# Attention and a split feed-forward on one core: order of a product's terms, tile starts on 128 bytes, a new program order

## The chip, the core and the metric

The kernel runs on one core of a Trainium2 chip. The core has TensorE (PE in the profile; its weight loads are shown apart as PEld), VectorE (DVE), ScalarE (ACT), GpSimd (POOL) and SyncE (SP, which here only issues transfers). The metric is the device time of one execution in microseconds, the median of a few runs. Before the change it was 241.62 us (three runs: 240.11, 241.62 and 242.28).

## The reference

What is computed, cut to its core. The attention is linear: both queries and keys are turned into products of two small projections, keys and values are summed once per batch, and queries read that sum. Its output, put together over heads, runs through a feed-forward with a squared relu.

```python
batch, n_heads, seq, head_dim, r = 4, 4, 1088, 32, 8      # 4352 tokens of 128 values
def phi(x):
    a = np.einsum('rd,bhsd->bhsr', S1, x)
    b = np.einsum('rd,bhsd->bhsr', S2, x)
    return np.einsum('bhsi,bhsj->bhsij', a, b).reshape(*x.shape[:-1], r * r)
q_p, k_p = (phi(q), phi(k))
kv = np.einsum('bhsf,bhsd->bhfd', k_p, v)
z = np.sum(k_p, axis=2)
num = np.einsum('bhsf,bhfd->bhsd', q_p, kv)
den = np.einsum('bhsf,bhf->bhs', q_p, z)[..., None] + 1e-06
x = (num / den), heads side by side                        # 4352 x 128
h = x @ w_in                                               # w_in 128 x 2048
g = s * np.maximum(h, 0.0) ** 2 + b
out = g @ w_out                                            # w_out 2048 x 128
```

## The kernel before

**Tiles.** Everything is held with the 128 features on the partitions and tokens along the free dimension. The 4352 tokens are cut into nine tiles (`TILES`): tile 0 of 256 tokens, tiles 1 to 8 of 512. The 2048 hidden columns are cut into eight pairs (`NPAIR`) of two blocks of 128.

**Keys.** `kvphase(b)` (k0 to k3 in the program order, one per batch) projects the keys (L247), transposes them on DVE (L251), multiplies the two projections (L254), sums keys times values on PE (L268), copies the sum (`kvt`), turns it (L283) and copies it to `st`.

**Queries.** `direct_features` (q0, q1) and `stored_features` (q2 to q8) make the query products `pq`; the latter go through DRAM (`qd`) to be spread over partitions. `attend(t)` (n0 to n8) multiplies them with `st` (L368), divides by the denominator on DVE (L381 to L397) and leaves the tile `x`. For tiles 1 to 8 it is split into a rounded part `xh` and the rest `xl`, both in fp32r, a form of fp32 that PE takes in one pass.

**Weights.** `split_weights` (w0 to w7, w0 the first 512 columns of `w_in`, w1 the first 512 rows of `w_out`, and so on by turns) turns 64-bit numbers from DRAM into fp32 in four steps, `to_float`: two scalings (L115/L117 and L121/L123, on DVE or ACT), a join and a sign step on DVE (L187, L183). The result, `w24`, is then split into large and small parts: `wih` and `wil` of `w_in`, `woh` and `wol` of `w_out`.

**Feed-forward.** `ffn(t, jp)` (the tokens 00 to 87 in the program order: tile, pair) has two matmul blocks. The first, hp, multiplies two weight blocks with x: for tiles 1 to 8 three fp32r matmuls each (small weights with `xh`, large weights with `xh`, large weights with `xl`), six in all, of 128x512. Then the tile `u` is made: relu out of PSUM (L129 on ACT or L127 on DVE), square (L135 or L133), rounding to `uh` (L111, either engine), and the rest `ul` = u - uh (L440, always DVE). The second block, ops, adds both weight blocks' three products into the output's PSUM tile, which is held over all eight pairs: `wol` with `uh`, `woh` with `uh`, `woh` with `ul`. Tile 0 is computed with fp32 matmuls, unsplit. `finish` (L500, L502) scales and stores a tile.

**Buffers.** hp has two PSUM buffers (`ps_h`), `u` two, `uh` and `ul` three each. A matmul stands in PE's program order and waits there for what it reads; DVE and ACT, too, work in program order.

**What sets the order.** `ORDER` is a table of tokens. Each names a generator (a load `L..`, `s`, k, q, n, w, a feed-forward pair, or `z`, one bf16 matmul that only keeps PE busy) and runs it up to its next `yield`. The table thus fixes every engine's order and the order of transfers on SP's queue. `ON_DVE` names the steps that run on DVE and not on ACT: a letter for the step (r relu, q square, u rounding to `uh`, x rounding to `xh`, w.. a weight step, a, b, k copies) and the place.

**Where tiles lie.** Tiles of the pool `const` lie one behind another in SBUF in the order in which they are made, then the pools p1, p2, p3 and p4. `sk` (80 fp32 numbers, 320 bytes for each partition) is followed by `sq`, `srep`, `kvt`, the four split weight tiles, `bias`, the eight `w24` and `s_bits` (320 bytes again). All of those after `sk` begin 64 bytes past a multiple of 128; after `s_bits` the two odd halves add up, and `st` and all tiles of p1 to p4 (`u`, `uh`, `ul`, `x`, `xh`, `xl` among them) begin on multiples of 128.

Of the kernel before, what the change touches and what calls it, by code (L numbers as in the profile page):

```python
# [19 lines left out]
P = 128  # L20
# [14 lines left out]
DEN_APART = (0,)  # L35
FIRST_F32 = (0, 1, 2, 3, 4, 5, 6, 7)
ORDER = """
Ls Lk0 Lk0 Lq0 Lk0 s s Lv0 s s Lv0 s z z z z z z k0 s s Lv0 k0 Lcst k0 z k0 Lq1 q0 q0 Lq2 k0 q0 Lw3 k0 z k0
Lw0 Lw1 k0 k0 z k0 Lw2 k0 q0 q0 Lw4 q0 k0 Lw6 Lw5 q1 k0 k0 q1 Lq4 k0 q1 q2 k0 q1 Lq3 q1 w3 q2 q1 w3 z n0 n0 n0
q2 w0 n0 n0 w0 n0 n0 n0 Lk1 w1 w0 z z z z z n1 w1 w0 Lw7 w3 w2 z 00 w2 w1 01 00 w1 Lq6 00 w2 01 00 w2 Lv1 01  # L40
w3 02 w4 n1 w4 n1 01 Lv1 02 n1 w4 w6 03 02 w6 w4 02 03 w5 w3 03 04 q2 w5 w6 03 Lk1 w0 04 q2 w6 q2 05 w5 04 w1
06 w5 05 w0 04 w6 w7 05 n1 07 n1 06 n1 05 06 n1 w3 n1 k1 w1 w7 q3 07 n1 10 07 w7 Lv3 q3 w7 w4 q3 11 k1 w7 w4
w5 06 w2 w2 07 10 k1 k1 07 07 12 10 k1 07 k1 q3 k1 10 q3 q3 11 Lk2 k1 Lk2 10 10 k1 Lv2 k1 11 Lv2 12 k1 11 14
k1 11 12 11 12 w5 q2 14 13 12 14 12 14 13 n2 14 13 15 w6 13 n2 n2 16 n2 13 15 15 n2 13 n2 n2 15 n2 17 w7 16 15
14 n2 16 17 15 n2 16 q3 20 17 16 Lk3 17 16 20 17 21 20 23 20 Lv3 21 17 20 21 23 22 17 Lk3 21 23 20 17 21 23 21
22 23 24 22 25 22 24 22 24 22 25 24 23 25 24 24 25 n3 25 25 n3 n3 n3 26 n3 n3 n3 27 26 n3 q4 26 n3 k2 n3 q4
Lq5 30 27 26 Lq7 q4 26 27 26 k2 30 k2 k2 30 31 k2 q4 27 30 q4 32 30 q4 30 k2 27 k2 32 k2 31 32 27 k2 32 k2 34
31 27 k2 32 27 31 33 k2 31 34 31 33 34 32 34 33 35 34 33 36 33 35 33 35 q4 36 35 34 35 n4 36 35 n4 36 n4 n4 37
n4 36 36 n4 37 n4 n4 37 q5 n4 k3 n4 37 41 k3 q5 37 q5 37 41 k3 42 37 41 37 40 q5 42 41 q5 q5 41 42 43 42 40 k3
42 q7 40 45 k3 43 40 q6 k3 43 44 q6 40 q7 q6 40 45 q7 41 q5 45 43 q6 42 q6 q6 43 45 n5 45 44 43 q7 44 n5 q7 n5  # L50
46 q7 n5 n5 44 n5 47 n5 46 n5 44 n5 k3 46 n5 q6 k3 46 47 50 46 k3 47 k3 44 50 45 50 47 46 50 47 47 50 50 q7 47
47 k3 51 k3 52 51 51 53 52 51 n6 52 51 51 52 53 n6 54 n6 53 n6 n6 52 55 53 54 n6 52 53 54 56 55 n6 55 53 54 54
54 55 56 57 55 56 n6 55 57 n6 n6 57 56 62 56 56 57 62 57 61 62 60 61 62 61 64 62 n7 61 60 61 57 60 n7 64 60 63
Lq8 60 57 60 57 64 63 61 n7 63 n7 n7 n7 62 n7 n7 64 n7 65 n7 64 66 63 65 q8 63 63 66 65 64 q8 66 65 q8 67 66
66 70 65 q8 65 q8 70 67 67 q8 66 67 70 71 67 70 67 70 72 71 67 71 70 72 67 71 73 72 71 72 71 73 q8 75 72 73 n8
73 72 75 73 75 n8 74 n8 n8 75 n8 n8 73 74 75 76 74 n8 n8 n8 74 77 76 74 74 76 n8 76 81 77 76 75 77 81 82 77 81
80 77 81 76 81 80 77 80 82 82 80 85 80 77 83 77 82 82 80 83 85 83 81 83 82 85 84 83 85 86 85 84 84 87 86 84 83
84 84 86 87 85 87 86 86 87 86 87 87 87 87 87 87
"""
# [30 lines left out]
def attn_ffn_kernel(ctx: ExitStack, tc: tile.TileContext, qT, kT, vp, s80, cst, w_in, w_out, outT):  # L90
    nc = tc.nc
    PSUM = bass.MemoryType.PSUM
    const = ctx.enter_context(tc.tile_pool(name="const", bufs=1))
# [115 lines left out]
    s_col = cst_sb[:, CS:CS + 1]  # L209
    b_col = cst_sb[:, CB:CB + 1]  # L210
    spread = cst_sb[:, CT:CT + P]
    sk = const.tile([P, NS], F32, name="sk")
    sq = const.tile([P, 64], F32, name="sq")
    srep = const.tile([P, 2, 64], F32, name="srep")

    def s_phase():
        bits = const.tile([P, NS], I32, name="s_bits")
        yield from to_float("s", sk, s_raw, bits)
        own = sk[:, 64:].rearrange("p (w r) -> p w r", w=2)
        nc.vector.tensor_copy(out=srep[:, 1].rearrange("p (i x) -> p i x", i=R),  # L220
                              in_=own[:, 1].unsqueeze(1).broadcast_to([P, R, R]))
# [222 lines left out]
    def product(out, terms, first=True, last=True):
        for k, (w, x) in enumerate(terms):
            nc.tensor.matmul(out, w, x, start=(first and k == 0), stop=(last and k == len(terms) - 1))  # L446

    def ffn(t, jp):
        _, N, _ = tiles[t]
        single = t == 0 and jp in FIRST_F32  # L450
        W = N + 2 if t == 0 else N
        hp = ps_h.tile([P, 2, 512], F32, name="hp")
        for i in range(2):
            c, c24 = columns(2 * jp + i)
            if single:
                product(hp[:, i, :N], ((w24[jp // 2, 0][c24], x_first[0]),))
            else:
                xh, xl = (x[:, :N] for x in xhl[t])
                product(hp[:, i, :N], ((wil[:, c], xh), (wih[:, c], xh), (wih[:, c], xl)))
        yield  # L460
        u = p2.tile([P, 2, NMAX], F32, name="u")
        if t == 0:
            nc.gpsimd.tensor_copy(out=u[:, :, N:W], in_=b_col.unsqueeze(2).broadcast_to([P, 2, 2]))
        relu(f"r{t}{jp}", u[:, :, :N], hp[:, :, :N])
        yield
        squared(f"q{t}{jp}", u[:, :, :N], u[:, :, :N])
        yield
# [109 lines left out]
```

## Time and profile before

| what | value |
|---|---|
| median of three runs | 241.62 us |
| profiled execution, whole | 241.27 us |
| its span, first to last instruction | 239.5 us |
| PE busy | 233.2 us, 97% of the span |
| DVE busy | 201.2 us, 84% |
| ACT busy | 174.5 us, 73% |
| granted TensorE clock, mean | 0.997 |

Sums and differences below are made against the profiled execution (241.27 us; 1.77 us of it lie outside of the span). It stands 0.35 us under the median. In the rows, L446 is the helper `product`, which issues every feed-forward matmul, and L111 the helper `copy`, so groups are told apart by the tiles' names: `hp<-xh,wil` is the first block, `ops<-ul,woh` the second. A matmul of fp32 (not fp32r) shows as two records.

### The profile page before, as it was taken

The numbers are of one execution on the slowest core, as the hardware profiler recorded it, in microseconds if no ns is written. First come the engines' busy times: TensorE is split into PE (matmuls) and PEld (weight loads), VectorE is DVE, ScalarE is ACT, GpSimd is POOL, SyncE is SP. The second block draws the span as 40 slices with busy tenths as digits, with TensorE's granted clock in tenths as the row PEclk, the third lists the DMA queues.
The fourth block names the chain that finished last, engine by engine and source line by source line (L and its number), as shares of the span: only waits on it lengthen the run. The fifth ranks groups of instructions, "written<-read, shape, count | busy, mean of one in ns | idle before, by whom it ended". The sixth has DMA issues, their size and how long they took to land.

```text
span 239.5 us, 4351 instructions
## 1 busy us (share of the span) xinstructions
PE 233.2 (97%) x1752; PEld 178.7 (75%) x1752; DVE 201.2 (84%) x262; ACT 174.5 (73%) x206; POOL 3.9 (2%) x15
## 2 busy tenths in 40 slices
PE   7999999999999999999999999999999999999993
PEld 3647877878887778877767887888687877888782
DVE  3679999999677899998998684999899896799882
ACT  2198986989987276856778976865955689987571
POOL 1000110000000000000000000000000000000000
PEclk9999999999999999999999999999999999999998
DMA  6999934870020053100356732000010510001001
GB/s 164 362 414 394 224 95 103 174 269 3 0 88 0 5 155 86 44 0 3 114 150 161 138 79 88 4 0 0 0 47 22 153 66 3 0 0 45 0 3 44
DMA packets 9812, 22.15 MB, mean 92 GB/s; under 512 B 1088, under 2 KB 3520, under 8 KB 9792
## 3 DMA queue, kind: packets, MB, share of 16 engines
q1 hardware_dynamic: 9792, 21.87, 30.7%
q8 instruction: 14, 0.23, 0.4%
q14 instruction: 6, 0.05, 0.1%
HBM read 18.72 MB, written 3.15 MB: 91 GB/s over the span
## 4 chain that ended last, share of the span: by engine, by line
PE 95%; DVE 2%; DMA 1%; ACT 1%; issue 0%; ACTq 0%; DVEq 0%
PE ops L446 41%; PE hp L446 40%; PE psa L368 4%; PE psa L268 4%; PE psa L247 2%; PE psa L327 2%; PE hp L307 1%; PE psa L283 1%; PE ops L512 1%; DMA s_raw<-s 1%; DVE w L187 0%; ACT u L129 0%; DVE pq L316 0%; ACT ot L500 0%; DVE rr L390 0%
## 5 line engine op out<-in xcount | busy, mean ns | idle before, releaser
L440 DVE TENSOR_TENSOR ul<-u,uh 128x1024 fp32r<-128x1024 f32 x64 | 77.9, 1221 | 12.7 <-ACT uh L111 10.2
L129 ACT ACTIVATE u<-hp 128x1024 f32<-128x1024 f32 (+1 forms) x62 | 60.0, 968 | 30.4 <-DVE ul L440 14.6
L135 ACT ACTIVATE u<-u 128x1024 f32<-128x1024 f32 (+1 forms) x53 | 53.6, 1012 | 8.7 <-DVE u L127 7.3
L446 PE MATMUL hp<-xh,wil 128*128 128x512 f32 x128 | 51.5, 402 | 0.0
L446 PE MATMUL ops<-uh,wol 128*128 128x512 f32 x128 | 51.1, 400 | 0.0
L446 PE MATMUL ops<-uh,woh 128*128 128x512 f32 x128 | 50.2, 392 | 0.0
L446 PE MATMUL hp<-xl,wih 128*128 128x512 f32 x128 | 50.2, 392 | 0.0
L446 PE MATMUL hp<-xh,wih 128*128 128x512 f32 x128 | 50.1, 392 | 0.0
L111 ACT CAST uh<-u 128x1024 fp32r<-128x1024 f32 x35 | 36.5, 1048 | 6.5 <-DVE u L133 3.3
L446 PE MATMUL ops<-ul,woh 128*128 128x512 f32 x128 | 39.9, 393 | 0.0
L446 PEld LDWEIGHTS hp<-xh,wil 128*128 128x128 f32 x128 | 24.0, 188 | 7.9 <-ACT u L129 1.4
L446 PEld LDWEIGHTS ops<-uh,wol 128*128 128x128 f32 x128 | 24.0, 188 | 7.5 <-issue 1.8
L446 PEld LDWEIGHTS hp<-xl,wih 128*128 128x128 f32 x128 | 24.0, 188 | 5.5
L446 PEld LDWEIGHTS ops<-ul,woh 128*128 128x128 f32 x128 | 23.8, 188 | 5.7 <-DVE ul L440 0.3
L446 PEld LDWEIGHTS ops<-uh,woh 128*128 128x128 f32 x128 | 24.1, 188 | 4.9
L446 PEld LDWEIGHTS hp<-xh,wih 128*128 128x128 f32 x128 | 24.1, 188 | 4.7
L111 DVE CAST uh<-u 128x1024 fp32r<-128x1024 f32 x29 | 20.0, 691 | 4.0 <-ACT u L135 3.1
L133 DVE TENSOR_TENSOR u<-u 128x1024 f32<-128x1024 f32 (+1 forms) x19 | 22.1, 1164 | 0.2
L127 DVE TENSOR_SCALAR u<-hp 128x1024 f32<-128x1024 f32 x10 | 12.2, 1223 | 4.1 <-PE hp L446 3.6
L254 DVE TENSOR_TENSOR ph<-kab 128x768 f32<-128x768 f32 (+2 forms) x9 | 11.0, 1221 | 0.2
L368 PE MATMUL psa<-pq,st 64*32 64x256 f32 (+3 forms) x320 | 10.2, 345 | 0.5 <-DVE x L397 0.5
L346 DVE TENSOR_TENSOR pq<-pq,br 128x1024 f32<-128x1024 f32 x7 | 8.5, 1220 | 2.0 <-DMA br<-qd 1.9
(63 smaller groups left out, 178.6 us busy)
## 6 DMA issues: line engine op xcount, KB each, us to landing
pq<-qd SPq DMA_DIRECT2D x7, 512.0 KB
br<-qd SPq DMA_DIRECT2D x14, 256.0 KB
qt<-qT SPq DMA_DIRECT2D x8, 256.0 KB
raw<-w_out SPq DMA_DIRECT2D x4, 512.0 KB
raw<-w_in SPq DMA_DIRECT2D x4, 512.0 KB
outT<-ot SPq DMA_DIRECT2D x7, 256.0 KB
vt<-vp SPq DMA_DIRECT2D x3, 330.0 KB
kt<-kT SPq DMA_DIRECT2D x3, 320.0 KB
```

What stands on the lines that cost most here:

```text
L111: (nc.vector.tensor_copy if key in ON_DVE else nc.scalar.copy)(out=out, in_=in_)
L127: nc.vector.tensor_scalar(out=out, in0=in_, scalar1=0.0, scalar2=None, op0=ALU.max)
L129: nc.scalar.activation(out=out, in_=in_, func=AF.Relu)
L133: nc.vector.tensor_tensor(out=out, in0=in_, in1=in_, op=ALU.mult)
L135: nc.scalar.activation(out=out, in_=in_, func=AF.Square)
L247: nc.tensor.matmul(ps[32 * q:32 * q + 32, w * w32:(w + 1) * w32], sk[:, 32 * w:32 * w + 32], kt[:, a:a + w32], start=(w == 0), stop=(w == ...
L254: nc.vector.tensor_tensor(out=ph[:, c0:c0 + n].rearrange("p c h i x -> p (c h) i x"), in0=a.unsqueeze(3).broadcast_to([P, H * n, R, R]), i ...
L268: nc.tensor.matmul(kvp[64 * g:64 * g + VW, 64 * j:64 * j + 64], v_in[b][:, c, h], ph[:, c, h].rearrange("p i x -> p (i x)"), start=(c == 0 ...
L346: nc.vector.tensor_tensor(out=pq, in0=pq, in1=br, op=ALU.mult)
L368: nc.tensor.matmul(out[32 * h:32 * h + 32, e0:e1], st_t[b][64 * r:64 * r + 64, h // 2, h % 2, y], pq[64 * r:64 * r + 64, h, e0:e1], start= ...
L440: nc.vector.tensor_tensor(out=ul[:, :, :N], in0=u[:, :, :N], in1=f32(uh[:, :, :N]), op=ALU.subtract)
L446: nc.tensor.matmul(out, w, x, start=(first and k == 0), stop=(last and k == len(terms) - 1))
```

## The change

Three things. The three products of a weight block are issued in another order in both blocks: small weights with the large stream, large weights with the small stream, then both large; in the second block this goes weight block by weight block, where before both products with `ul` stood last. `sk` and `s_bits` get 96 columns in memory (384 bytes) of which 80 are used, so that every tile of const and of the pools begins on a multiple of 128 bytes. And `ORDER` and `ON_DVE` are new: 745 tokens for 746 (one z fewer; all else the same set), and 70 steps on DVE for 71 (among the large ones 15 relus for 10, 17 squares for 17, 28 roundings to `uh` for 29).

```diff
-Ls Lk0 Lk0 Lq0 Lk0 s s Lv0 s s Lv0 s z z z z z z k0 s s Lv0 k0 Lcst k0 z k0 Lq1 q0 q0 Lq2 k0 q0 Lw3 k0 z k0
...
+z z z z z z z z Ls Lk0 Lq0 Lk0 Lcst s s Lk0 s s Lv0 s s s Lv0 k0 Lv0 q0 Lq1 q0 k0 k0 k0 Lw0 Lq2 k0 Lw2 k0 z k0
...
 ON_DVE = frozenset("""
-a8 k20 k21 k31 q02 q03 q11 q16 q31 q32 q33 q36 q41 q54 q62 q64 q65 q70 q71 q80 q81 q85 q86 r11 r23 r25 r26 r33
...
+a4 a6 b00 k01 q02 q10 q12 q13 q21 q34 q45 q51 q53 q63 q65 q67 q71 q72 q80 q81 q85 q86 r15 r21 r23 r24 r31 r42
...
-    sk = const.tile([P, NS], F32, name="sk")
+    sk = const.tile([P, 96], F32, name="sk")[:, :NS]
...
-        bits = const.tile([P, NS], I32, name="s_bits")
+        bits = const.tile([P, 96], I32, name="s_bits")[:, :NS]
...
-                product(hp[:, i, :N], ((wil[:, c], xh), (wih[:, c], xh), (wih[:, c], xl)))
+                product(hp[:, i, :N], ((wil[:, c], xh), (wih[:, c], xl), (wih[:, c], xh)))
...
-                terms += [(wol[:, c], uh[:, i, :W]), (woh[:, c], uh[:, i, :W])]
-        if not single:
-            for i in range(2):
-                c, _ = columns(2 * jp + i)
-                terms.append((woh[:, c], ul[:, i, :W]))
+                terms += [(wol[:, c], uh[:, i, :W]), (woh[:, c], ul[:, i, :W]), (woh[:, c], uh[:, i, :W])]
```

Two places show how instructions stand. The first is on DVE near the start, from the query products of tile 1 to the first weight tile (`w_00` is w0 as fp32, `x` the output of n0). Before:

```order
L316 TENSOR_TENSOR pq<-hp,br 128x2x128 x2
L316 TENSOR_TENSOR pq<-hp,br 128x512
L115 TENSOR_SCALAR w_11_98<-raw_182 128x512
L316 TENSOR_TENSOR pq<-hp,br 128x512
L377 STREAM_TRANSPOSE dt<-hp 128x256
L384 TENSOR_SCALAR rc<-dt 128x8
L387 RECIPROCAL rc<-rc 128x8
L390 STREAM_TRANSPOSE rr<-rc 128x256
L397 TENSOR_TENSOR x<-psa,rr 128x128 x2
L187 SCALAR_TENSOR_TENSOR w_00_95<-w_00_95,raw_195 128x512
L183 SCALAR_TENSOR_TENSOR w_00_95<-raw_195,w_00_95 128x512
```

and after the change, on DVE again:

```order
L316 TENSOR_TENSOR pq<-hp,br 128x2x128 x2
L111 COPY kvt_86<-psa 33x256
L115 TENSOR_SCALAR w_00_95<-raw_178 128x512
L121 TENSOR_SCALAR raw_178<-raw_178 128x512
L187 SCALAR_TENSOR_TENSOR w_00_95<-w_00_95,raw_178 128x512
L316 TENSOR_TENSOR pq<-hp,br 128x512
L183 SCALAR_TENSOR_TENSOR w_00_95<-raw_178,w_00_95 128x512
L316 TENSOR_TENSOR pq<-hp,br 128x512
L377 STREAM_TRANSPOSE dt<-hp 128x256
```

All four steps of w0 now stand on DVE ahead of the steps of n0 that make x; before, two of them ran on ACT and the other two came behind x. The second place is on PE at the same time, the attend step of tile 1 (`psa<-pq,st ... 32x256`) and the first feed-forward matmuls. Before:

```order
L368 MATMUL psa<-pq,st_284 32x256 x16
L512 LDWEIGHTS const-bfloat16-1.0
L512 MATMUL ops<-const-bfloat16-1.0 128x512
L446 MATMUL hp<-x,w_00_95 128x256 x4
L446 MATMUL ops<-u,w_01_96 128x258 x2
L446 MATMUL hp<-x,w_10_97 128x256 x2
```

and after the change, on PE:

```order
L446 MATMUL hp<-x,w_00_95 128x256 x4
L368 MATMUL psa<-pq,st_290 32x256 x16
L446 MATMUL ops<-u,w_01_96 128x258 x2
L446 MATMUL hp<-x,w_10_97 128x256 x4
L446 MATMUL ops<-u,w_01_96 128x258 x2
```

The first two pairs of tile 0 now stand ahead of the attend step of tile 1.

## Rows read from the trace of the kernel before

**Rows 1.** The page, part 1 and the transfer rate of part 2 (40 slices of 5.99 us)

```profile
PE 233.2 (97%) x1752; PEld 178.7 (75%) x1752; DVE 201.2 (84%) x262; ACT 174.5 (73%) x206; POOL 3.9 (2%) x15
...
GB/s 164 362 414 394 224 95 103 174 269 3 0 88 0 5 155 86 44 0 3 114 150 161 138 79 88 4 0 0 0 47 22 153 66 3 0 0 45 0 3 44
```

**Rows 2.** Windows: stretch, length, busy of PE, PEld, DVE, ACT, POOL, then granted clock

```profile
0.00:32.60 32.60, 30.20 (x357) 19.63 (x357) 24.41 (x50) 21.95 (x42) 3.87 (x15) 1.00 0.90 298
32.60:235.40 202.80, 202.80 (x1400) 159.03 (x1396) 176.75 (x213) 151.52 (x163) 0.00 (x0) 1.00 0.22 60
```

**Rows 3.** Timeline of PE in mid-run: start us, length us, line, operation

```profile
101.99 0.39 PE L446 MATMUL hp<-xh,wil 128*128 128x512 f32 x1
...
103.37 0.39 PE L446 MATMUL ops<-uh,wol 128*128 128x512 f32 x1
```

**Rows 4.** Timeline of PE, start of the feed-forward, with a run of bf16 matmuls

```profile
14.83 1.26 PE L512 MATMUL ops<-const-bfloat16-1.0 128*128 128x512 bf16 x5
16.57 1.29 PE L368 MATMUL psa<-pq,st 64*32 64x256 f32 x32 [0.47 <-DVE x L397]
17.79 0.39 PE L512 MATMUL ops<-const-bfloat16-1.0 128*128 128x512 bf16 x1
18.20 1.99 PE L446 MATMUL hp<-x,w 128*128 128x256 f32 x8
20.73 1.11 PE L446 MATMUL ops<-u,w 128*128 128x258 f32 x4 [0.54 <-DVE w L187]
```

**Rows 5.** Timeline of PE and its weight loads around one late `ul`

```profile
192.04 0.40 PE L446 MATMUL ops<-uh,woh 128*128 128x512 f32 x1
192.29 0.73 PE L446 MATMUL ops<-ul,woh 128*128 128x512 f32 x2
...
191.82 0.19 PEld L446 LDWEIGHTS ops<-uh,woh 128*128 128x128 f32 x1
192.28 0.30 PEld L446 LDWEIGHTS ops<-ul,woh 128*128 128x128 f32 x2 [0.28 <-DVE ul L440]
```

**Rows 6.** Groups by line and shape: count, busy us, mean ns, idle before

```profile
L440 DVE TENSOR_TENSOR ul<-u,uh 128x1024 fp32r<-128x1024 f32 x64 | 77.9, 1221 | 12.7 <-ACT uh L111 10.2
L129 ACT ACTIVATE u<-hp 128x1024 f32<-128x1024 f32 x54 | 55.3, 1024 | 29.4 <-DVE ul L440 14.6 <-PE hp L446 12.3 <-PE ops L446 1.6
...
L135 ACT ACTIVATE u<-u 128x1024 f32<-128x1024 f32 x47 | 49.9, 1061 | 8.5 <-DVE u L127 7.3
L111 ACT CAST uh<-u 128x1024 fp32r<-128x1024 f32 x35 | 36.5, 1048 | 6.5 <-DVE u L133 3.3 <-PE psa L368 2.4
...
L127 DVE TENSOR_SCALAR u<-hp 128x1024 f32<-128x1024 f32 x10 | 12.2, 1223 | 4.1 <-PE hp L446 3.6
```

**Rows 7.** Timeline of DVE and PE at the end of the run

```profile
232.15 2.56 DVE L440 TENSOR_TENSOR ul<-u,uh 128x1024 fp32r<-128x1024 f32 x2
...
234.01 0.39 PE L446 MATMUL ops<-uh,wol 128*128 128x512 f32 x1
...
234.93 0.62 PE L446 MATMUL ops<-ul,woh 128*128 128x512 f32 x2
```

**Rows 8.** Timeline of DVE near the start

```profile
13.20 0.69 DVE L316 TENSOR_TENSOR pq<-hp,br 128x512 f32<-128x512 f32 x1 [2.35 <-ACT br L111]
13.81 0.42 DVE L115 TENSOR_SCALAR w<-raw 128x512 f32<-128x512 f32 x1
...
16.22 0.49 DVE L397 TENSOR_TENSOR x<-psa,rr 128x128 f32<-128x128 f32 x2
16.63 0.80 DVE L187 SCALAR_TENSOR_TENSOR w<-w,raw 128x512 int32<-128x512 int32 x1
17.46 0.69 DVE L183 SCALAR_TENSOR_TENSOR w<-raw,w 128x512 int32<-128x512 int32 x1
```

**Rows 9.** Timeline of ACT near the start, seven weight steps, then the first relu

```profile
14.26 0.71 ACT L123 ACTIVATE raw<-raw 128x512 int32<-128x512 uint32 x1
...
17.77 0.68 ACT L123 ACTIVATE raw<-raw 128x512 int32<-128x512 uint32 x1
19.37 0.60 ACT L129 ACTIVATE u<-hp 128x512 f32<-128x512 f32 x1 [0.92 <-PE hp L446]
```

More of the change, by code (lines that the diff above doesn't have):

```diff
@@ L37 @@
 ORDER = """
-Ls Lk0 Lk0 Lq0 Lk0 s s Lv0 s s Lv0 s z z z z z z k0 s s Lv0 k0 Lcst k0 z k0 Lq1 q0 q0 Lq2 k0 q0 Lw3 k0 z k0
[L39 to L57, printed above, removed]
@@ L58 @@
-84 84 86 87 85 87 86 86 87 86 87 87 87 87 87 87
+z z z z z z z z Ls Lk0 Lq0 Lk0 Lcst s s Lk0 s s Lv0 s s s Lv0 k0 Lv0 q0 Lq1 q0 k0 k0 k0 Lw0 Lq2 k0 Lw2 k0 z k0
+Lw5 Lw1 k0 Lw3 k0 z k0 k0 Lw4 q0 k0 Lw6 q0 q0 q0 q1 k0 k0 q1 Lv2 w0 k0 q1 w0 Lk1 q2 w0 k0 q1 q1 q2 w0 Lk1 w2 z
+n0 q1 n0 w2 n0 w0 Lv1 n0 w5 n0 n0 w5 n0 n0 w5 Lv1 w1 z z z z 00 w2 w1 01 00 w1 Lq3 n1 00 w1 w3 w5 w3 00 Lw7 w2
+w4 w3 02 w4 q2 01 w3 01 03 w4 Lq4 w3 w4 01 02 n1 w2 02 04 w1 n1 02 03 w1 03 w0 05 04 n1 n1 03 n1 04 w6 n1 04
+Lk2 n1 05 w6 k1 05 w6 q3 n1 w6 q2 05 w7 q2 n1 w7 q2 k1 06 w6 w7 w5 07 w7 06 k1 k1 06 10 07 07 k1 w7 k1 06 w4
@@ new lines @@
+q3 07 w7 10 q3 w3 k1 07 10 07 07 k1 w6 Lk3 Lk3 w2 11 q3 k1 10 k1 q3 q3 10 13 11 w5 11 12 q2 11 w4 k1 10 12 11
+k1 11 13 12 13 12 14 12 13 n2 13 14 15 14 n2 n2 16 15 14 12 Lq7 15 n2 n2 14 13 n2 16 15 17 16 15 16 n2 14 n2
+17 n2 n2 15 17 16 20 17 q3 21 17 20 20 23 21 20 16 21 20 17 21 23 22 17 21 23 17 26 22 23 20 23 22 24 22 26 22
+26 25 24 Lk2 21 24 22 26 26 23 25 27 24 25 24 n3 25 Lv2 24 27 25 27 n3 25 n3 n3 n3 n3 26 n3 n3 q4 n3 k2 27 n3
+30 q4 27 q4 31 30 k2 k2 30 k2 27 q4 31 30 q4 q4 k2 32 31 30 27 30 31 32 27 k2 k2 32 31 32 k2 32 35 k2 Lv3 k2
@@ new lines @@
+Lv3 q4 k2 35 33 35 34 35 31 k2 35 34 n4 Lq6 33 34 32 33 n4 n4 34 37 33 34 36 33 37 Lq5 33 n4 37 n4 n4 36 n4 34
+n4 n4 36 n4 35 q5 36 q6 37 41 q5 37 q5 42 41 36 q6 36 41 42 q5 41 q5 40 q5 42 q6 41 37 42 40 k3 42 40 q7 k3 43
+37 k3 q7 37 44 43 40 40 43 46 q7 q5 44 40 q6 q6 44 q6 41 n5 43 43 42 q7 n5 q7 46 n5 43 q7 44 46 n5 n5 45 n5 46
+n5 n5 47 44 n5 n5 45 44 46 50 45 47 k3 47 45 51 45 47 45 k3 50 47 50 46 k3 51 47 50 51 k3 47 50 47 k3 51 50 k3
+k3 51 k3 q7 51 k3 q6 52 53 52 52 55 53 52 n6 53 54 52 53 55 n6 52 53 Lq8 55 n6 53 n6 n6 54 n6 56 55 n6 n6 n6
@@ new lines @@
+55 n7 54 57 n6 56 n7 54 56 60 54 56 54 57 n7 n7 56 55 57 n7 n7 60 62 n7 n7 60 57 61 57 60 56 62 n7 n7 62 64 60
+62 57 61 q8 62 61 63 61 57 64 60 57 61 64 63 61 q8 q8 63 62 64 66 63 64 q8 65 63 66 q8 q8 63 66 65 66 64 65 66
+67 65 70 67 65 71 67 70 65 70 67 67 72 71 q8 66 71 67 70 71 70 73 67 71 72 67 70 73 72 74 73 72 76 72 74 n8 73
+71 74 73 75 74 n8 n8 76 n8 72 n8 n8 76 n8 77 n8 n8 74 76 73 n8 75 76 74 75 77 81 75 77 75 80 77 75 80 77 76 80
+81 77 81 80 80 82 77 77 81 83 82 81 82 84 83 82 80 82 83 85 84 83 81 83 84 85 82 84 85 86 84 85 87 85 86 83 86
@@ L59 @@
+87 84 87 86 86 85 87 87 86 87 87 87 87 87
 """
 ON_DVE = frozenset("""
-a8 k20 k21 k31 q02 q03 q11 q16 q31 q32 q33 q36 q41 q54 q62 q64 q65 q70 q71 q80 q81 q85 q86 r11 r23 r25 r26 r33
-r45 r52 r70 r81 r85 u11 u14 u21 u22 u26 u30 u35 u40 u41 u42 u47 u52 u54 u55 u56 u57 u60 u61 u62 u63 u65 u66
-u71 u74 u80 u82 u83 u84 u86 w2h w3m w5h w5m w7m x3 x4 x6 x7
+a4 a6 b00 k01 q02 q10 q12 q13 q21 q34 q45 q51 q53 q63 q65 q67 q71 q72 q80 q81 q85 q86 r15 r21 r23 r24 r31 r42
+r51 r53 r61 r62 r63 r65 r74 r77 r84 u10 u15 u22 u23 u24 u26 u31 u34 u36 u37 u40 u42 u43 u44 u45 u51 u54 u57
@@ L64 @@
+u61 u64 u65 u67 u70 u72 u73 u81 u82 u86 w0b w0m w6b x2 x4
 """.split())
```

## The prediction

> **What bounds the kernel now.** I read the busy times first, then busy time by stretch, then the timeline of PE, and last the two vector engines where PE takes their results. The page has PE at 97% and DVE at 84% [rows 1]. The windows cut the run in two. From 32.6 us, where the first fp32r matmul starts, to 235.4 us, where the last ends, PE has 202.80 us of work in 202.80 us [rows 2]; DVE fills 176.75 of them, 87%. So behind 32.6 us TensorE alone sets the time, and a faster vector engine would buy nothing there. Ahead of it lie 32.6 us in which PE is filled in part by bf16 matmuls that compute nothing, and at the end 4.1 us for the last scaling and store.
>
> What is PE's work? In mid-run six matmuls of 128x512 take 103.37 - 101.99 = 1.38 us, 0.230 each [rows 3]. There are 768 of them: 8 tiles, 8 pairs, 12 each. That is 176.6 of the 202.8 us; the rest are the small matmuls of attention set between. Records overlap (each is 0.39 long), so the pace is read from starts, never from lengths. The bf16 matmuls of the same width and at the same granted clock, 1.00 in both windows [rows 2], go faster: five in 1.26 us, the last one 0.39 long, so (1.26 - 0.39) / 4 = 0.2175 each [rows 4]. An fp32r matmul thus costs 0.0125 us more than the clock asks for, 768 x 0.0125 = 9.6 us in all. Whether the change touches that is its largest question.
>
> **The change part by part.**
>
> *Tile starts.* No instruction is added or removed. What moves is where the weights begin: `wih`, `wil`, `woh`, `wol` and `w24` go from 64 past a multiple of 128 bytes onto one. The streams (`x`, `xh`, `xl`, `u`, `uh`, `ul`) lay on multiples of 128 before and move by 128. For a gain, reading the weights must be what slows the stream. One matmul speaks on that: the one at 192.04 has no weight load beside it, since the load before it began at 191.82 and took 0.19, and the next began at 192.28, held up by a late `ul` [rows 5]. It still took 0.40, where its neighbours with a load took 0.39. With nothing loading, the stream was no faster, so I put this part at 0. Its ends are -9.6 us, if all of the gap closes, and, since nothing excludes it, a loss of some of that size if the new starts are worse for the stream.
>
> The rule that speaks for the gap comes from the Trainium skill, TensorE: Matmul & The Clock Gate, section "Back-to-back issue gap": N / 2.4 + 2.5 ns between warm matmuls, 216 ns for 512 columns. The bf16 row agrees and the fp32r row, 0.230, does not; by the page's figure the 768 would take 166 us and not 177. Against the change speaks the box on "cachelines" in SBUF — State Buffer: lines are 16 bytes and the price is for crossing them, so that a start 64 bytes off is as good as one on 128. No row here has weights on 128 in fp32r, so neither is shown.
>
> *Order of terms.* The same six matmuls stand in a block, with the same six weight loads, so PE's work is equal. Only the need moves: the first product with `ul` goes from the fifth to the second place, and `ul` must be there 3 x 0.23 = 0.69 us earlier. With the old program order this would hurt. At the very end `ul` is ready at 232.15 + 2.56 = 234.71, for a matmul at 234.93 [rows 7]; in second place, with the block starting at 234.01, it would be asked for at 234.24 and be 0.47 late. The new order gives this back. I counted, in both programs, the fp32r matmuls between the last of a pair's first block and its first use of `ul`: on average 32.9 before and 37.1 after, at least 16 before and 19 after; pairs with fewer than 30 were 31 of 64 and are 11. In time, 4.2 x 0.23 = 1.0 us more slack on average, with the earlier need counted in. The chain that must fit is relu 1.02, square 1.06, rounding 1.05, rest 1.22, together 4.35 us [rows 6]; 19 matmuls are 4.37 us, without the small groups that may stand between. So four pairs have no slack to spare and the others have. I put this at 0; its ends are 0 and what the second rival prices. (`xl` is needed 0.23 us earlier too, once a tile, at most 8 x 0.23 = 1.8 us; I take 0, as n now ends further ahead of its use.)
>
> *Moved steps.* Five more relus on DVE are 5 x 1.22 = 6.1 us [rows 6]; the other moved steps go mostly the other way, so this is an upper bound. DVE then has 176.75 + 6.1 = 182.9 of 202.8 us, 90%. Hidden behind PE, 0; if that cover goes, the price is the second rival's. Small groups between fp32r matmuls: I count 21 stretches in both programs, so nothing is saved or added. One z fewer: it filled idle time, 0.
>
> *The start.* Here the order moves the end, because everything behind it is PE's work without a gap. Before, x was ready at 16.22 + 0.49 = 16.71, but w0's last step ended only at 17.46 + 0.69 = 18.15 [rows 8], and the first feed-forward matmul started at 18.20. Meanwhile PE ran the attend step of tile 1, from 16.57, and one bf16 matmul; the second block of pair 0 came at 20.73, after 0.54 idle [rows 4]. After, w0's four steps stand on DVE ahead of x. They cost 0.42 + 0.42 + 0.80 + 0.69 = 2.33 us (the second is not seen on DVE; I take its sister's 0.42, at most the join's 0.80), and DVE sat idle for 2.35 us up to 13.20 [rows 8]. A small copy of `kvt` comes in, and the 0.42 step of `w_11` leaves. So they fit into the gap if w0's numbers have landed by 13.20 - 2.35 = 10.85. On SP's queue 1.76 MB now stand ahead of w0's 0.52 MB; at the rates of the first two slices, 164 and 362 GB/s [rows 1], 0.98 MB land in 5.99 us and the other 1.30 MB in 3.6 us, 9.6 us in all. In time, then, and x stays at 16.71. The first two pairs run at once, some 1.75 us, then the attend step, 1.2: PE is ready for pair 0's second block at 19.7. What it needs: seven ACT steps from 14.3 at (17.77 - 14.26) / 6 = 0.585 [rows 9], 18.4; then relu and square, 1.2 us, 19.6; and behind the last of the seven, w1's join and sign step on DVE, 0.80 + 0.69, 19.9. So 19.9 against 20.73, a gain of 0.8 us. From there to 38 us both vector engines are close to full in either program, and I keep the 0.8. Its ends: -1.7, if the idle spells that follow go too, and +0.8, if w0's 2.33 us are not covered and x comes at 19.0.
>
> Sum against the profiled execution: 241.27 - 0.8 = 240.5; the median stands 0.35 above that execution, so **240.8 us**.
>
> **The rivals.**
>
> *The stream speeds up with its weights on 128 bytes.* For it: the gap of 0.0125 us exists and only fp32r shows it, which reads four bytes a column in one pass. Against it: the matmul without a load beside it [rows 5]. If it all closes, 240.8 - 9.6 = 231.2 us; DVE with up to 182.9 of then 193 us would still hold.
>
> *`ul` comes late; slower.* The wait that the old order of terms had behind it moves to the second place of a block, and PE stands there, with all later matmuls queued behind. For it: DVE gets relus of 1.22 us in front of `ul` steps, and the old run ended with 0.22 us of slack [rows 7]. It decides where a pair has fewer than 30 matmuls between: 11 pairs. At 0.47 us each, as at the end of the old run, that is 5.2 us: 246.0 us. Against it: the four tightest pairs just fit, and before the change 31 pairs had fewer than 30 and PE did not stop once for long.
>
> *The start gains more.* PE's 32.6 us at the start hold 2.4 us idle [rows 2], and several bf16 fillers. If the new order closes these, 3 us in all: 238.3 us.
>
> **How the numbers follow.** Forecast 0.65, its own range 239.3 to 242.6; faster stream 0.12; late `ul` 0.12; larger gain at the start 0.11. Faster or slower counts from 1%, 2.4 us, about what runs of this kernel can tell from no change. Faster: all of the first rival, most of the third and a little of the forecast, 0.23. Slower: the second and a little of the forecast, 0.14. Same: 0.63. The range leaves out the faster stream and the far half of the late `ul`: 237.4 to 244.6.
>
> **What would show it.** Right: fp32r starts still 0.230 apart; the first feed-forward matmul near 16.8 and the first fp32r matmul's stretch some 0.8 us shorter up to the same work; PE without idle behind it; waits for `ul` below 0.5 us in total. Wrong: starts 0.217 apart; weight loads that wait for `ul` in many blocks; or DVE idle near 11 us, waiting for w0's transfer, and x late.

## The result, and the profile after

The changed kernel takes 243.93 us (median of four runs, 243.38 to 244.38), the kernel before 241.34 us in its four. The ratio is 1.0112, with a 95% interval of 1.0073 to 1.0150: slower by about 1%. The profiled execution of the changed kernel took 243.94 us, its span is 242.2 us: 2.67 us more than the 241.27 us of before.

The busy times, part 1 of the page of the changed kernel (answers to [rows 1]):

```profile
PE 234.4 (97%) x1751; PEld 178.6 (74%) x1751; DVE 203.9 (84%) x261; ACT 174.2 (72%) x207; POOL 4.1 (2%) x15
```

and its windows, in the columns of [rows 2]; here the second stretch runs from the first fp32r matmul to the end of the last:

```profile
0.00:32.60 32.60, 29.19 (x355) 19.01 (x355) 26.26 (x54) 22.24 (x42) 4.08 (x15) 1.00 0.85 295
33.20:237.90 204.70, 204.62 (x1384) 159.25 (x1380) 177.07 (x208) 150.31 (x163) 0.00 (x0) 1.00 0.22 60
```

PE is full behind the start, as before, at the same granted clock of 1.00. DVE has 177.07 of 204.70 us, 86%. No new wait shows; the stretch of full PE has only become longer. What has changed is seen where PE runs fp32r matmuls alone, with no small group between them. The longest such run of the changed kernel has 149 of them; these are the first and the last start of it, from the timeline of PE (start us, length us; to be held against [rows 3]):

```profile
203.04 0.39 PE L446 MATMUL ops<-ul,woh 128*128 128x512 f32 x1
...
237.51 0.40 PE L446 MATMUL ops<-uh,woh 128*128 128x512 f32 x1
```

34.47 us for 148 steps are 0.2329 each; [rows 3] had 0.230. Over all starts that have an fp32r matmul on either side and come within 0.26 us of the one ahead, some 720 of the 768, the mean is 0.2293 before and 0.2326 after. The difference, 0.0033 us, times 768 is 2.5 us: nearly the whole loss of 2.67.

The start, timeline of PE ([rows 4]):

```profile
17.21 1.99 PE L446 MATMUL hp<-x,w 128*128 128x256 f32 x8 [1.06 <-DVE x L397]
19.13 1.09 PE L368 MATMUL psa<-pq,st 64*32 64x256 f32 x32
20.16 1.14 PE L446 MATMUL ops<-u,w 128*128 128x258 f32 x4
...
22.45 1.13 PE L446 MATMUL hp<-x,w 128*128 128x256 f32 x4 [0.30 <-ACT u L129]
23.42 1.03 PE L446 MATMUL ops<-u,w 128*128 128x258 f32 x4
...
32.63 0.64 PE L247 MATMUL psa<-kt,sk 128*32 128x128 f32 x16
33.20 0.50 PE L446 MATMUL hp<-xh,wil 128*128 128x512 f32 x1
```

The new order stands as planned: pairs 0 and 1 ahead of the attend step, the second block of pair 0 at 20.16 and not at 20.73. But the first fp32r matmul starts at 33.20, where it was 32.59, with the 16 matmuls of L247 now ahead of it, 0.57 us. The other matmuls ahead of it are the same in both traces but for one z, so at equal work it is 32.63: nothing is gained. Two places show where the lead was lost. On DVE ([rows 8]):

```profile
11.86 0.43 DVE L115 TENSOR_SCALAR w<-raw 128x512 f32<-128x512 f32 x1 [0.52 <-DMA raw<-w_in]
12.21 0.42 DVE L121 TENSOR_SCALAR raw<-raw 128x512 int32<-128x512 uint32 x1
12.66 0.70 DVE L187 SCALAR_TENSOR_TENSOR w<-w,raw 128x512 int32<-128x512 int32 x1
...
16.67 0.49 DVE L397 TENSOR_TENSOR x<-psa,rr 128x128 f32<-128x128 f32 x2
```

w0's numbers landed at 11.86, and DVE waited 0.52 us for them; x was ready at 17.16, not at 16.71. And on ACT ([rows 9]):

```profile
18.38 0.60 ACT L129 ACTIVATE u<-hp 128x512 f32<-128x512 f32 x1 [0.60 <-PE hp L446]
...
19.54 0.69 ACT L117 ACTIVATE w<-raw 128x512 f32<-128x512 f32 x1
...
21.25 0.68 ACT L123 ACTIVATE raw<-raw 128x512 int32<-128x512 uint32 x1
21.81 0.59 ACT L129 ACTIVATE u<-hp 128x512 f32<-128x512 f32 x1
```

four weight steps stand between the first relu and the second, where before none stood (19.37 and 20.54), so pair 1 has its relu at 21.81, and PE waits for it at 22.45.

The groups that the change moves ([rows 6]), by line and shape:

```profile
L440 DVE TENSOR_TENSOR ul<-u,uh 128x1024 fp32r<-128x1024 f32 x64 | 77.9, 1220 | 7.9 <-ACT uh L111 5.6 <-PE hp L446 1.1
...
L127 DVE TENSOR_SCALAR u<-hp 128x1024 f32<-128x1024 f32 x15 | 18.3, 1223 | 8.2 <-PE hp L446 7.4
```

Fifteen relus at 1.223, as costed. The second block, which reads `ul`, has no line for it among the waits of PE's weight loads. What the view puts down to `ul` (us in total, times, longest) stands at the first block and the attend step, which don't read it:

```profile
PEld hp L446 <- DVE ul L440: 0.8, 2, 0.4
...
PEld psa L368 <- DVE ul L440: 0.4, 1, 0.4
```

At the end the last fp32r matmul starts 4.7 us ahead of the span's end, where it was 4.3.

### The profile page after: what moved, and what is told of

The parts are those of the page before. It is cut to its first block, busy times and chain, and to the rows that moved or that the text cites. A ratio compares the mean times of both kernels' runs of the same rounds, so it can differ in the third digit from the quotient of the medians.

```text
span 242.2 us, 4323 instructions
## 1 busy us (share of the span) xinstructions
PE 234.4 (97%) x1751; PEld 178.6 (74%) x1751; DVE 203.9 (84%) x261; ACT 174.2 (72%) x207; POOL 4.1 (2%) x15
## 4 chain that ended last, share of the span: by engine, by line
PE 92%; DVE 3%; ACT 3%; issue 1%; ACTq 0%; DVEq 0%
PE ops L446 40%; PE hp L446 40%; PE psa L368 3%; PE psa L268 3%; PE psa L247 2%; PE ops L508 1%; PE psa L327 1%; PE hp L307 1%; ACT u L129 1%; PE psa L283 1%; DVE ph L254 1%; DVE pq L316 1%; ACT raw L123 0%; ACT w L117 0%; DVE kab L251 0%
## 5 line engine op out<-in xcount | busy, mean ns | idle before, releaser
L129 ACT ACTIVATE u<-hp 128x1024 f32<-128x1024 f32 (+1 forms) x57 | 54.8, 964 | 23.5 <-PE hp L446 13.1
L135 ACT ACTIVATE u<-u 128x1024 f32<-128x1024 f32 (+1 forms) x54 | 54.3, 1006 | 7.4 <-DVE u L127 6.0
L446 PE MATMUL ops<-ul,woh 128*128 128x512 f32 x128 | 50.5, 395 | 0.0
L111 ACT CAST uh<-u 128x1024 fp32r<-128x1024 f32 x36 | 37.8, 1050 | 9.2 <-PE ops L446 5.1
L127 DVE TENSOR_SCALAR u<-hp 128x1024 f32<-128x1024 f32 x15 | 18.3, 1223 | 8.2 <-PE hp L446 7.4
L133 DVE TENSOR_TENSOR u<-u 128x1024 f32<-128x1024 f32 (+1 forms) x18 | 21.4, 1193 | 1.8 <-ACT u L129 1.5
L111 DVE CAST uh<-u 128x1024 fp32r<-128x1024 f32 x28 | 19.1, 684 | 4.2 <-PE ops L446 2.4
L496 ACT ACTIVATE ot<-ops,bias,cst_sb 128x512 f32<-128x512 f32 (+1 forms) x10 | 7.0, 709 | 6.2 <-PE ops L446 6.2
```

What stands on the lines that cost most here:

```text
L111: (nc.vector.tensor_copy if key in ON_DVE else nc.scalar.copy)(out=out, in_=in_)
L496: nc.scalar.activation(out=ot[:, s], in_=o[:, s], func=AF.Identity, scale=s_col, bias=bias)
```

## The experiments

The theory: the new tile starts slow the fp32r matmuls. Rivals: the order of terms (T in the texts) or the new program order (O) does it. In the texts below, written before each run, the theory of the tile starts is A; its later forms are P (the distance between a weight's and a stream's start counts) and W (the weights' own start counts). Paces are means over some 720 starts unless an unbroken run is named.

### The three parts alone

**e1_align**, only the tile starts:

```diff
-    sk = const.tile([P, NS], F32, name="sk")
+    sk = const.tile([P, 96], F32, name="sk")[:, :NS]
-        bits = const.tile([P, NS], I32, name="s_bits")
+        bits = const.tile([P, 96], I32, name="s_bits")[:, :NS]
```

> The kernel before with sk and s_bits padded to 384 bytes and nothing else. Theory A (the new starts of the weights slow the fp32r stream): mean start-to-start of fp32r matmuls 0.2326 us as in the changed kernel, not 0.2293 as before; 768 x 3.3 ns = 2.5 us more, 243.9 us. Theory T (the order of the terms slows it) and theory O (the program order costs the time): pace 0.2293, 241.3 us.

**e2_terms**, only the order of terms:

```diff
-                product(hp[:, i, :N], ((wil[:, c], xh), (wih[:, c], xh), (wih[:, c], xl)))
+                product(hp[:, i, :N], ((wil[:, c], xh), (wih[:, c], xl), (wih[:, c], xh)))
...
-                terms += [(wol[:, c], uh[:, i, :W]), (woh[:, c], uh[:, i, :W])]
+                terms += [(wol[:, c], uh[:, i, :W]), (woh[:, c], ul[:, i, :W]), (woh[:, c], uh[:, i, :W])]
```

> The kernel before with the new order of terms alone, old program order, old tile starts. Theory T: pace 0.2326. Theories A and O: pace 0.2293, and waits for ul at the pairs with little slack in the old order, 0.47 us at each of some ten pairs, so 243 to 246 us by waits and not by pace.

**e3_order**, only the new `ORDER` and `ON_DVE`:

```diff
-Ls Lk0 Lk0 Lq0 Lk0 s s Lv0 s s Lv0 s z z z z z z k0 s s Lv0 k0 Lcst k0 z k0 Lq1 q0 q0 Lq2 k0 q0 Lw3 k0 z k0
...
+z z z z z z z z Ls Lk0 Lq0 Lk0 Lcst s s Lk0 s s Lv0 s s s Lv0 k0 Lv0 q0 Lq1 q0 k0 k0 k0 Lw0 Lq2 k0 Lw2 k0 z k0
...
```

> The kernel before with the new ORDER and ON_DVE alone, old terms, old tile starts. Theory A: pace 0.2293 and the earlier start kept, 0.5 to 0.9 us under the kernel before, 240.6 us. Theory O: 243.9 us at whatever pace. Theory T: as theory A.

**e4_unaligned**, the changed kernel without its new tile starts:

```diff
-    sk = const.tile([P, 96], F32, name="sk")[:, :NS]
+    sk = const.tile([P, NS], F32, name="sk")
-        bits = const.tile([P, 96], I32, name="s_bits")[:, :NS]
+        bits = const.tile([P, NS], I32, name="s_bits")
```

> The changed kernel with sk and s_bits back at 320 bytes, so that weights begin 64 past a multiple of 128 again. Theory A: pace 0.2293, 243.9 - 2.5 = 241.2 us or a little less. Theory T: pace stays 0.2326 and the time 243.9. Theory O: 243.9.

| kernel | us | ratio to before (240.87 us) | pace, us |
|---|---|---|---|
| e1_align | 243.52 | 1.0132 [1.0088, 1.0175] | 0.2326 |
| e2_terms | 246.13 | 1.0225 [1.0183, 1.0267] | 0.2297 |
| e3_order | 241.17 | 1.0028 [1.0009, 1.0047] | 0.2293 |
| e4_unaligned | 241.34 | 1.0023 [1.0000, 1.0046] | 0.2294 |

The tile starts alone make the loss, and without them the changed kernel stands within 0.3% of before. The text of e3_order was right in the pace and wrong in the time: it expected 0.5 to 0.9 us less than before, and the kernel took 0.3 us more. The same unbroken run of 149 matmuls, timeline of PE of e4_unaligned:

```profile
201.16 0.40 PE L446 MATMUL ops<-ul,woh 128*128 128x512 f32 x1
...
235.08 0.39 PE L446 MATMUL ops<-uh,woh 128*128 128x512 f32 x1
```

33.92 / 148 = 0.2292, against 0.2329 with the new starts, in the same program order. And in e1_align, a run of 114:

```profile
204.03 0.39 PE L446 MATMUL ops<-uh,woh 128*128 128x512 f32 x1
...
230.29 0.43 PE L446 MATMUL hp<-xh,wil 128*128 128x512 f32 x1
```

26.26 / 113 = 0.2324. The same 114 in the kernel before:

```profile
201.18 0.39 PE L446 MATMUL ops<-uh,woh 128*128 128x512 f32 x1
...
227.06 0.45 PE L446 MATMUL hp<-xh,wil 128*128 128x512 f32 x1
```

25.88 / 113 = 0.2290.

The order of terms alone is worse than the whole change, and by waits, not by pace. The waits of PE's weight loads in e2_terms (us in total, times, longest):

```profile
PEld ops L446 <- DVE ul L440: 7.0, 15, 0.9
```

and one of them on the timeline, PE and then DVE:

```profile
178.77 0.40 PE L446 MATMUL ops<-uh,wol 128*128 128x512 f32 x1
179.67 0.50 PE L446 MATMUL ops<-ul,woh 128*128 128x512 f32 x1 [0.50 <-DVE ul L440]
...
178.40 1.22 DVE L440 TENSOR_TENSOR ul<-u,uh 128x1024 fp32r<-128x1024 f32 x1
```

`ul` is ready at 179.62; in fifth place, at 178.77 + 4 x 0.23 = 179.69, it would just have been in time; in second place PE stands for 0.67 us. The new program order takes these waits away: with it, the new order of terms (e4_unaligned) and the old one (e3_order) take the same time, 241.34 and 241.17 us.

### Which starts are bad

The next six kernels are the kernel before with tiles moved. A weight slice is 128 columns of 4 bytes, 512 bytes, so the distance from the stream's start to the weight's is the same for every matmul of a kernel, taken modulo 512. Four of the six change the two sizes A and B:

```diff
-    sk = const.tile([P, NS], F32, name="sk")
+    sk = const.tile([P, A], F32, name="sk")[:, :NS]
-        bits = const.tile([P, NS], I32, name="s_bits")
+        bits = const.tile([P, B], I32, name="s_bits")[:, :NS]
```

with A, B = 96, 80 (**e5_w0_s64**), 80, 96 (**e6_w64_s64**), 104, 88 (**e7_w32**) and 88, 104 (**e8_w96**).

> The kernel before with sk at 384 and s_bits at 320 bytes: weights on multiples of 128, streams 64 past one. Theory W (the weights' own start sets the pace): 0.2326 us per fp32r matmul, 243.5 us. Theory P (the distance between a weight's start and a stream's, modulo 128, sets it; it is 64 again here): 0.2293, 241 us.

> The kernel before with sk at 320 and s_bits at 384 bytes: weights and streams both 64 past a multiple of 128. Theory W: 0.2293, 241 us. Theory P (distance 0, as in the changed kernel): 0.2326, 243.5 us.

> The kernel before with weights 32 past a multiple of 128 and streams on one (sk 416, s_bits 352 bytes). Both theories leave this open: if half the distance does half of the work, 0.231; if only whole lines of 64 bytes count, the pace of one of the two ends, 0.2293 or 0.2326; if 64 was not the best place, less than 0.2293.

> The kernel before with weights 96 past a multiple of 128 and streams on one (sk 352, s_bits 416 bytes). As for 32: 0.231 if the effect goes by degrees, one of 0.2293 and 0.2326 if it goes by lines, less if a better place exists; a difference between 32 and 96 would say that the direction counts.

These four fit a distance modulo 128: weights on 128 are no fault by themselves (e5), nor is 64 past it a virtue (e6). Theory W falls. The texts of e7 and e8 offered 0.231, one of the two ends, or less than 0.2293; measured were 0.2334 and 0.2342, worse than either end. But all fast kernels had 448 modulo 512, so the modulus was not shown. Two later kernels move the streams alone, by 128 (**e17_shift128**) and by 256 bytes (**e18_shift256**), with a tile that holds nothing (32 columns of 4 bytes here, 64 in e18):

```diff
+    pad = const.tile([P, 32], F32, name="pad")
     w24 = {(i, k): const.tile([P, CW], F32, name=f"w24_{i}{k}") for i in range(DFF // CW) for k in range(2)}
```

> Kernel before with 128 bytes of padding behind the split weight tiles, so that the streams move by 128: distance 64 modulo 128 as in the kernel before, but 320 and not 448 modulo 512 (the bytes of one weight slice of 128 columns). In the runs up to here the two were tied: all fast kernels have 448 modulo 512, all kernels with 0 modulo 128 have 384. If the distance counts modulo 128: 0.2293 and 241.1 us. If it counts modulo 256 or 512: slower, 0.231 to 0.234, 242.5 to 244 us.

> The same with 256 bytes of padding: distance 64 modulo 128, 192 modulo 256 as before, and 192 modulo 512. Counts modulo 128 or 256: 0.2293 and 241.1 us. Counts modulo 512: slower, 0.231 to 0.234.

An unbroken run of 114 in each, timeline of PE, e17_shift128 first:

```profile
201.93 0.40 PE L447 MATMUL ops<-uh,woh 128*128 128x512 f32 x1
...
228.30 0.43 PE L447 MATMUL hp<-xh,wil 128*128 128x512 f32 x1
```

and e18_shift256:

```profile
200.24 0.40 PE L447 MATMUL ops<-uh,woh 128*128 128x512 f32 x1
...
226.12 0.46 PE L447 MATMUL hp<-xh,wil 128*128 128x512 f32 x1
```

26.37 / 113 = 0.2334 and 25.88 / 113 = 0.2290.

| weight start less stream start, modulo 512 (256) | kernels | pace, us | ratio to before |
|---|---|---|---|
| 448 (192) | before, e2 to e5 | 0.2293 to 0.2297 | e5: 1.0024 [0.9996, 1.0053] |
| 192 (192) | e18_shift256 | 0.2295 | 0.9990 [0.9964, 1.0015] |
| 384 (128) | after, e1, e6 | 0.2325, 0.2326 | e6: 1.0081 [1.0051, 1.0111] |
| 320 (64) | e17_shift128 | 0.2333 | 1.0074 [1.0049, 1.0098] |
| 416 (160) | e7_w32 | 0.2334 | 243.41 us, one run |
| 352 (96) | e8_w96 | 0.2342 | 243.54 us, one run |

So P holds with another modulus than its first texts say: 64 modulo 128 isn't enough (e17), 192 modulo 256 is (e18). That the modulus is 256 rests on one pair of distances modulo 512, 448 and 192; the others have no such partner. Neither start decides alone: e5 (0.2294) and e6 (0.2325) have their streams in the same places, and before, e18 (0.2293, 0.2295), e6 and e17 (0.2325, 0.2333) their split weights. The change moved this distance from 192 to 128.

Four kernels tried to go finer: each split weight tile gets 32 more columns and is used from a later one.

```diff
-    wih = const.tile([P, DFF], F32R, name="wih")
+    wih = const.tile([P, DFF + 32], F32R, name="wih")[:, 20:20 + DFF]
```

for all four tiles, with 20 columns (**e13_d16**), 28 (**e14_d48**), 4 (**e15_d80**) and 12 (**e16_d112**).

> Kernel before with the four split weight tiles 16 past a multiple of 128 bytes, streams on one: distance 16. Theory of halves (what counts is in which 64-byte half of 128 the two start; opposite halves are good): same half, slow, 0.2325 to 0.2345. Theory of one good point (only 64 is good, everything else costs): slow too. If the pace falls off evenly with the distance from 64: 0.2325, by 0, 32 and 96, which were no better the closer they came, that is unlikely.

> Distance 48. Theory of halves: same half as the streams, slow, 0.2325 to 0.2345. One good point at 64: slow too. Even fall-off: about 0.2305. If a finer distance closes the gap to the bf16 pace, 0.2175.

> Distance 80. Theory of halves: the other half, good, 0.229; it already has 96 against it (0.2342). One good point at 64: slow, 0.2325 to 0.2345. Even fall-off: about 0.2305.

> Distance 112. Theory of halves: 0.229; one good point at 64: slow, 0.2325 to 0.2345; even fall-off: 0.2325.

They gave 0.2307, 0.2317, 0.2316 and 0.2320 (241.49, 242.55, 243.23 and 243.23 us, one run each, before 241.25). All lie between the rules' numbers, and the kernels were ill made for the question: a tile of 8,320 bytes puts the next one 128 further modulo 256, so each has two distances, 128 apart. Their texts, which count on one distance in each, don't apply, and they settle no rule.

### Is it the weight load beside the stream?

**e9_narrow_d64** is the kernel before, **e10_narrow_d0** is e1_align, and in both the middle products of a block are computed for 32 of the 128 weight columns only (one of three in hp, four of six in ops; that part of the output is left out):

```diff
-            nc.tensor.matmul(out, w, x, start=(first and k == 0), stop=(last and k == len(terms) - 1))
+            m = 32 if 0 < k < len(terms) - 1 and w.dtype == F32R else P
+            nc.tensor.matmul(out[:m], w[:, :m], x, start=(first and k == 0), stop=(last and k == len(terms) - 1))
```

> Kernel before (64 bytes modulo 128 between a weight's start and its stream's), but the middle products of each block (one of three in hp, four of six in ops) are computed with 32 of 128 weight columns, so their weight load is a quarter and part of the output is left out. If the load of the next weights, which runs beside the stream, is what slows the stream (theory P: weights and stream meet in SBUF), a full-width matmul with a narrow load behind it starts its successor after less than 0.226 us, towards 0.2175, and one with a full load behind it after 0.229. If the 0.229 belongs to the fp32r stream itself (rival), both are 0.229 and only the distance of the starts matters for some other reason.

> The same with sk and s_bits padded (0 bytes modulo 128 between the starts): same part left out. Theory P: with a full load behind it a matmul keeps 0.2326, with a narrow one the difference to the kernel of the run before shrinks to a quarter, under 0.001 us, both towards 0.2175. Rival (the distance acts on the matmul without the load beside it, as by its own weights against its own stream): 0.2326 with narrow loads behind full-width matmuls too.

An unbroken run of 114 in each, timeline of PE, e9_narrow_d64 first:

```profile
202.13 0.40 PE L447 MATMUL ops<-uh,woh 128*32 128x512 f32 x1
...
228.35 0.43 PE L447 MATMUL hp<-xh,wil 128*128 128x512 f32 x1
```

and e10_narrow_d0:

```profile
202.87 0.39 PE L447 MATMUL ops<-uh,woh 128*32 128x512 f32 x1
...
228.90 0.42 PE L447 MATMUL hp<-xh,wil 128*128 128x512 f32 x1
```

Their paces are 26.22 / 113 = 0.2320 and 26.03 / 113 = 0.2304. With less to load the kernel before became slower (from 0.2290) and e1_align faster (from 0.2324). The narrow loads took 0.108 us, the full ones 0.188. Both texts were wrong: neither pace came near 0.2175, and one of them rose, so it isn't the amount that a load reads alone which slows the stream. Yet the streams were untouched, and the pace moved, in opposite directions in the two. A full matmul with a narrow load beside it (the first of a weight block in hp) went from 0.2291 to 0.2336 to its successor's start in e9 and from 0.2327 to 0.2281 in e10. So the load has a part in it, or the narrow successor has; these runs don't part the two. Total times were 242.61 and 243.09 us (one run each), before 240.74.

**e11_small_at0** and **e12_large_at0** give small and large weights different distances, by 64 bytes of padding between the four tiles (`pad1` to `pad4`, behind each tile in e11, ahead of it in e12):

```diff
     wih = const.tile([P, DFF], F32R, name="wih")
+    pad1 = const.tile([P, 16], F32, name="pad1")
     wil = const.tile([P, DFF], F32R, name="wil")
```

> Kernel before, but wil and wol begin on a multiple of 128 bytes (distance 0 to the streams) and wih and woh stay 64 past one (distance 64), by 64 bytes of padding between them. A matmul runs with its own weights already loaded, while the weights of the next are loaded. If the load beside the stream matters (theory P), a matmul's spacing to the next follows the NEXT matmul's weights: in hp xh,wih (next also wih) and xh,wil (next wih) stay at 0.229, xl,wih (next is wil, distance 0) goes to 0.2326; in all about 0.2305. If the matmul's own weights matter (rival), xh,wil goes to 0.2326 and the other two stay.

> The mirror image: wih and woh at distance 0, wil and wol at 64. Theory P: xh,wil (next wih) and xh,wih (next wih) go to 0.2326, xl,wih (next wil) stays at 0.229; in all about 0.2315. Rival, own weights: xh,wil stays, the other two go to 0.2326.

| mean spacing behind | small weights | large, next large | large, next small |
|---|---|---|---|
| e11_small_at0, us | 0.2305 | 0.2324 | 0.2328 |
| e12_large_at0, us | 0.2331 | 0.2321 | 0.2312 |

The rival (own weights) has the wrong sign in both. Theory P has the signs right where small weights are the own or the next ones, but large next large, which it put at 0.229 in e11, is at 0.2324. Modulo 256 the padding gave the four tiles four distances, so this design could not answer. The times were 243.54 and 242.51 us (one run each), before 241.03. Whether the load of the next weights or the matmul's own pair decides is open.

## Why the prediction was wrong

The forecast was a small gain, with less than 1% of change as the likeliest outcome, and the kernel is 1.1% slower by a mechanism that had no rival of its own. That the time still lies in the range is luck: its upper end was taken from the late `ul`, which did not come.

**Tile starts: the step that failed.** The step was "With nothing loading, the stream was no faster, so I put this part at 0". It measured +2.5 us (768 x 0.0033; e4_unaligned to the changed kernel is +2.45 us in the profiled executions). The inference read [rows 5] by the length of a record, 0.40 against 0.39. One record's length doesn't show the pace: after the change the records are 0.39 and 0.40 too, while their starts have moved from 0.2292 to 0.2329 apart. The prediction itself had said that the pace is read from starts, never from lengths, and then this step used a length. The same trace of before had no second placement to compare, so a loss was bounded ("of some of that size") but not priced: it should have been a rival with a chance, since the streams moved by 128 and the weights by 64, which changes their distance whatever the right rule is.

The Trainium skill, SBUF — State Buffer, box on "cachelines", has lines of 16 bytes and a price for crossing into a new one; by that a start 64 bytes off would be as good as one on 128. Here the starts were not of equal worth, and neither was good by itself: e5, with weights on 128 and streams 64 off, and e6, with both 64 off, run at 0.2294 and 0.2325. The Trainium skill, TensorE: Matmul & The Clock Gate, section "Step-by-step: what each phase is for", says that loading the next weights takes no read bandwidth from the running matmul. e9 and e10 agree as to the amount: less to load slowed the one and quickened the other. From e4_unaligned to the changed kernel the pace moved by 0.0032 with the same loads, and only tiles lay elsewhere; by what way this acts, no run here shows.

**Faster stream, rival one.** Wrong in its sign: the starts on 128 gave 0.2326, not 0.2175.

**Order of terms: right.** With the new program order it costs nothing (e3 to e4: 241.17 and 241.34 us), with the old one it hurts, as the step said. The second rival's price came out too, 15 waits, 7.0 us, 0.47 each in the mean, in part by luck: it was read from one pair, and the waits run up to 0.9. Only its condition was not met by the new order: 11 pairs with fewer than 30 matmuls between, and no wait for `ul` in their second block that shows. Counted again from the two program orders, the matmuls between are 32.7 before and 37.0 after in the mean, 32 pairs before had fewer than 30, and five pairs after, not four, have only 19; nothing rests on these differences. What PE loses net in e2_terms is less than the loads' waits, 246.13 - 240.87 = 5.3 us.

**Moved steps: right.** Five more relus of 1.223 us are there; DVE has 177.07 of 204.70 us, 86%, because the other moves gave back what the upper bound left out. PE is full beside it.

**The start: the term of -0.8 us measured 0.0.** It came in two parts. The transfer of w0 was put at 9.6 us, from mean rates, and landed at 11.86; x was 0.45 late for it, the sign of being wrong that the prediction had named. The second block of pair 0 still came 0.57 us earlier, at 20.16, so "I keep the 0.8" is what failed: four weight steps stood on ACT in front of the next relu, and from pair 1 on (23.42, where it was 22.54) the lead was gone. Moreover one execution can't tell this term: the same block starts at 19.69 to 21.67 us in the profiles of before, e1, e2 and e5 to e8, which share one order, and at 20.07 to 20.84 in the three with the new order.

**Sum.** First fp32r matmul at equal work 32.63 - 32.59 = 0.04; first to last start 204.30 - 202.57, plus the 0.57 of L247 that has moved out of it, 2.30; the end 4.66 - 4.32 = 0.34: 2.68 us, which is the difference of the two profiled executions, 2.67, but for rounding.

## What to carry to other kernels

Where TensorE is full with back-to-back matmuls, read its pace from first and last starts of an unbroken run, and price any edit that moves tiles in SBUF by it: 1.4% of the pace hung on the distance between weights and streams, and here rounding all tiles up to 128 bytes was worse than leaving the weights 64 off. Try two or three paddings, whose only cost is some bytes, and keep the distances of all weight tiles equal while doing so. An order of work that gives slack and an order of terms that spends it belong together: alone, the second cost 2.25% here.

## What was not expected of the hardware

The pace of fp32r matmuls is not a number of one matmul but a cycle of several. By the trace's starts in ns, the spacings before went 232, 226, 229 over and over, through hp and ops alike and whatever the operands were; after, 238, 229 in one stretch and a cycle of nine in another. And e13_d16 ran at two paces in one execution, timeline of PE, two unbroken runs:

```profile
49.72 0.39 PE L446 MATMUL hp<-xh,wih 128*128 128x512 f32 x1
...
74.88 0.61 PE L446 MATMUL ops<-ul,woh 128*128 128x512 f32 x2
...
200.83 0.40 PE L446 MATMUL ops<-uh,woh 128*128 128x512 f32 x1
...
227.20 0.42 PE L446 MATMUL hp<-xh,wil 128*128 128x512 f32 x1
```

The first has 112 matmuls to the start at 74.88, 25.16 / 111 = 0.2267, the second 114, 26.37 / 113 = 0.2334, at the same granted clock (1.00 in both), with the same weight tiles in use. 0.2267 is faster than the pace of any kernel here; held throughout it would give 768 x 0.0026 = 2.0 us, an estimate from these rows. It looks as if what starts a stretch chooses between cycles that the distance allows; that is not shown, and no kernel held the fast one throughout. Nor does a good distance hold its pace everywhere. e18_shift256, whose run of 114 has 0.2290, is slower right behind it, timeline of PE:

```profile
226.41 0.40 PE L447 MATMUL hp<-xh,wih 128*128 128x512 f32 x1
...
234.08 0.63 PE L447 MATMUL ops<-ul,woh 128*128 128x512 f32 x2
```

These are 34 matmuls to the start at 234.08, 7.67 / 33 = 0.2324, as slow as the changed kernel, and e2_terms has 41 matmuls from 99.69 to 109.00 at 9.31 / 40 = 0.2328. So the distance told the mean pace of a kernel, and not the pace of every stretch in it. No kernel here beats the one before: e18_shift256 is the nearest, at 0.9990 with an interval that holds 1.
